# Attention, then routed experts: requesting each expert's rows an expert earlier, moving two transposes, halving the last copy

## The chip, the cores and the metric

The kernel runs on one core of one Trainium2 chip. The metric is device time in microseconds (us) of one launch; lower is better. The core has a matrix engine (TensorE), two engines that read its accumulators (VectorE and ScalarE), GpSimd, which here issues most of the DMA transfers, and sixteen DMA engines. A profile ("trace") is of one execution. The span that it shows is shorter than the reported time of the same execution (250.5 and 252.12).

## The reference, cut to what matters

```python
def reference(**kwargs):
    attn_out = _attn_ref(q, k, v)                  # 8 batches x 8 heads x 576 x 64, keys and values pooled by 8
    x = attn_out.transpose(0, 2, 1, 3).reshape(4608, 512)
    return _moe_ref(x, domain_id, w1, w2)

def _moe_ref(x, domain_id, w1, w2):                # 8 experts, w1 512 x 1024, w2 1024 x 512
    for e in range(8):
        mask = domain_id == e
        h = np.maximum(x[mask] @ w1[e], 0.0)
        out[mask] = h @ w2[e]
```

Every token goes to exactly one expert. The kernel computes the attention, writes the rows x to device memory, and then works through the experts: it gathers the rows of one expert, transposes them, multiplies by w1, applies ReLU, multiplies by w2 and scatters the results to their tokens.

## The kernel before

An expert has room for 640 rows, five blocks of 128. Four kinds of work matter here. A *gather* of one block is an indirect DMA issued by GpSimd. There are two gather buffers, used by even and odd experts. A *turn* is the transposition of one or two gathered blocks on TensorE, followed by a copy to `xT`.

```python
    def gather(e, j, rows=XROWS):
        i = nc.gpsimd.indirect_dma_start(
            out=xg[e % 2][:, j, :], out_offset=None, in_=x_lin[0:rows, :],
            in_offset=bass.IndirectOffsetOnAxis(ap=xrow[:, NBL * e + j:NBL * e + j + 1], axis=0), ...)

    def turn_units(e, j0, j1, tag="big", step=2):
        def unit(a):
            ...
            for j in range(a, z):
                for kk in range(4):
                    nc.tensor.transpose(p[:, j - a, kk, :], xg[e % 2][:, j, 128 * kk:128 * kk + 128], ident[:])
            ...
                nc.vector.tensor_copy(dst, p[:, 0:z - a])      # dst is a part of xT of this expert
```

A *first layer* has eight units of up to eight matmuls; their results are copied to `hT`. A *second layer* has one unit of eight matmuls for each block of 128 rows, a copy to `y`, and a scatter that GpSimd issues.

```python
    def l2_units(e, s0, s1, hT):
        def unit(j):
            p = one(s0 // 128 + j)                             # a PSUM tile of 128 x 512 fp32
            for fi in range(8):
                nc.tensor.matmul(p, hT[:, fi, 128 * j:128 * j + 128], w2[:, fi, :], start=(fi == 0), stop=(fi == 7))
            y = late.tile([128, HD], F32, tag="y", bufs=8, name="y")
            flip[0] ^= 1
            if flip[0]:
                nc.vector.tensor_copy(y[:], p)
            else:
                nc.scalar.activation(y[:], p, AFT.Copy)
            ...                                                # scatter y to out by token, on GpSimd
```

The driver puts the units in order. `paced` interleaves gathers into a first layer: before each one, GpSimd reads one element of `hT`, so it can't run ahead of TensorE.

```python
        run(turn_units(0, 2, 3) + l1_units(0, a, b, h, a))
        run(l2_units(0, 0, b, h) + turn_units(0, 3, NBL))
        run(wload_units(2, 0, 1))
        for j in range(NBL):
            gather(2, j)
        run(l1_units(0, b, CAP, h, b))
        u = l2_units(0, b, CAP, h[:, :, b:CAP])
        t = turn_units(1, 0, NBL)
        run([t[0], u[0], t[1], u[1], t[2]] + wload_units(2, 1, 1))
        for e in range(1, E):
            h = hidden()
            u = l1_units(e, 0, CAP, h, 0)
            ...
            g = [lambda j=j: gather(e + 1, j) for j in range(NBL)] if 2 < e + 1 < E else []
            u = paced(u, h, 0, g, [0, 2, 3, 5, 6])
            run(merge(u, count() if e == 2 else []))
            u = l2_units(e, 0, CAP, h)
            t = turn_units(e + 1, 0, NBL) if e + 1 < E else [lambda: None] * 3
            w = wload_units(e + 2, 0, 1) + wload_units(e + 2, 1, 1) if e + 2 < E else [lambda: None] * 2
            run([u[0], w[0], u[1], t[0], u[2], w[1], t[1], u[3], t[2], u[4]])
```

The softmax here doesn't subtract the row's maximum and nothing guards it: scores larger than these inputs give would overflow.

Of the kernel before, what the change touches and what calls it, by code (L numbers as in the profile page):

```python
# [10 lines left out]
AFT = mybir.ActivationFunctionType  # L11
# [5 lines left out]
HD = 512  # L17
N = B * S
FF = 1024
E = 8  # L20
# [4 lines left out]
NBL = CAP // 128  # L25
# [42 lines left out]
def kernel(  # L68
# [10 lines left out]
    nc = tc.nc  # L79
# [30 lines left out]
    def one(i):  # L110

        if i % 3 != 2:
            return small()[:]
        return wide()[:].rearrange("p a b -> p (a b)")[:, 0:512]
# [24 lines left out]
    with tc.manual_schedule():  # L139
# [447 lines left out]
        def merge(a, b, start=0.0):  # L587

            out_, n = [], len(a)
            pos = [start * n + (i + 0.5) * (1 - start) * n / len(b) for i in range(len(b))] if b else []  # L590
            j = 0
            for i, x in enumerate(a):
                while j < len(b) and pos[j] <= i:
                    out_.append(b[j])
                    j += 1
                out_.append(x)
            return out_ + list(b[j:])
# [6 lines left out]
        def wload_units(e, which, parts):  # L604
            box = {}

            def unit(i):
                if i == 0:
                    tag = W_AT[e % 3][which]
                    k = (4, 8)[which]  # L610
                    t = wp.tile([128, 72, D], F16, tag=tag, bufs=2, name=tag)
                    box["t"] = t[:].rearrange("p t d -> p (t d)")[:, 0:4096].rearrange("p (k f) -> p k f", k=k)
                    box["s"] = (moe_w1, moe_w2)[which][e].rearrange("(k p) f -> p k f", k=k)
                    wt.setdefault(e, []).append(box["t"])
                n = (4, 8)[which] // parts
                nc.gpsimd.dma_start(box["t"][:, n * i:n * i + n], box["s"][:, n * i:n * i + n])
            return [lambda i=i: unit(i) for i in range(parts)]
# [3 lines left out]
# [3 lines that stand above are left out]
                in_offset=bass.IndirectOffsetOnAxis(ap=xrow[:, NBL * e + j:NBL * e + j + 1], axis=0),  # L624
                bounds_check=rows - 1, oob_is_err=False)
            tc.add_to_no_dep_group("xg", i.ins)

        def turn_units(e, j0, j1, tag="big", step=2):
            def unit(a):
                if a == 0:  # L630
                    xts[e] = per.tile([128, 4, CAP], F16, tag="xT", bufs=2, name="xT")
                z = min(a + step, j1)
                p = ps.tile([128, 2, 4, 128], F16, tag=tag, bufs=2, name="turn")
# [3 lines that stand above are left out]
                dst = xts[e][:, :, 128 * a:128 * z].rearrange("p k (j c) -> p j k c", c=128)  # L637
                if tag == "small":
                    nc.scalar.activation(dst, p[:, 0:z - a], AFT.Copy)
                else:  # L640
                    nc.vector.tensor_copy(dst, p[:, 0:z - a])  # L641
            return [lambda a=a: unit(a) for a in range(j0, j1, step)]

        flip = [0]
# [9 lines left out]
        def paced(u, hT, c, fs, at):  # L654
            out_ = []
            for fi, x in enumerate(u):
                out_.append(x)
                out_ += [pace(hT, fi, c, f) for f, i in zip(fs, at) if i == fi]
            return out_

        def hidden():
            return late.tile([128, 8, CAP], F16, tag="hT", bufs=2, name="hT")

        def l1_units(e, s0, s1, hT, h0, alone=False):
            n = s1 - s0
            xT = xts[e]
            w1 = wt[e][0]
            nh = 1 if n <= 512 else 2
            m = n // nh

            def unit(fi):
                p = two(None if alone else fi)
                for kk in range(4):
                    for a in range(nh):
                        nc.tensor.matmul(p[:, a, 0:m], w1[:, kk, 128 * fi:128 * fi + 128], xT[:, kk, s0 + m * a:s0 + m * a + m],  # L675
                                         start=(kk == 0), stop=(kk == 3))
                dst = hT[:, fi, h0:h0 + n].rearrange("p (a c) -> p a c", a=nh)
                if fi % 2 == 0 or alone:
                    nc.scalar.activation(dst, p[:, 0:nh, 0:m], AFT.Relu)  # L679
                else:  # L680
                    nc.vector.tensor_scalar(out=dst, in0=p[:, 0:nh, 0:m], scalar1=0.0, scalar2=None,  # L681
                                            op0=ALU.max)
            return [lambda fi=fi: unit(fi) for fi in range(8)]

        def l2_units(e, s0, s1, hT):
            w2 = wt[e][1]

            def unit(j):
                p = one(s0 // 128 + j)
                for fi in range(8):  # L690
                    nc.tensor.matmul(p, hT[:, fi, 128 * j:128 * j + 128], w2[:, fi, :],  # L691
                                     start=(fi == 0), stop=(fi == 7))
                y = late.tile([128, HD], F32, tag="y", bufs=8, name="y")
                flip[0] ^= 1
                if flip[0]:
                    nc.vector.tensor_copy(y[:], p)  # L696
                else:
                    nc.scalar.activation(y[:], p, AFT.Copy)  # L698
                bl = NBL * e + s0 // 128 + j
                i = nc.gpsimd.indirect_dma_start(  # L700
                    out=out, out_offset=bass.IndirectOffsetOnAxis(ap=orig[0][:, bl:bl + 1], axis=0),
                    in_=y[:], in_offset=None, bounds_check=N - 1, oob_is_err=False)
                tc.declare_no_dep(i.ins, group="ys", reason="each token has its own row")
                tc.add_to_no_dep_group("ys", i.ins)
            return [lambda j=j: unit(j) for j in range((s1 - s0) // 128)]

        def run(units):
            for f in units:
                f()
# [88 lines left out]
        def read_count():  # L798
            nonlocal nblk
            nblk = nc.values_load(nblk_i[0:1, 0:1], min_val=0, max_val=N // 128)  # L800

        a, b = [slots for slots, _ in EARLY]
        h = e0["hT"]
# [4 lines left out]
            gather(1, j)  # L808
        run(wload_units(1, 1, 1))
        run(turn_units(0, 2, 3) + l1_units(0, a, b, h, a))  # L810
        run(l2_units(0, 0, b, h) + turn_units(0, 3, NBL))
        run(wload_units(2, 0, 1))
        for j in range(NBL):
            gather(2, j)
        run(l1_units(0, b, CAP, h, b))
        u = l2_units(0, b, CAP, h[:, :, b:CAP])
        t = turn_units(1, 0, NBL)
        run([t[0], u[0], t[1], u[1], t[2]] + wload_units(2, 1, 1))
        for e in range(1, E):
            h = hidden()  # L820
            u = l1_units(e, 0, CAP, h, 0)
            if e == E - 1:
                nc.gpsimd.drain()
            g = [lambda j=j: gather(e + 1, j) for j in range(NBL)] if 2 < e + 1 < E else []
            u = paced(u, h, 0, g, [0, 2, 3, 5, 6])
            run(merge(u, count() if e == 2 else []))
            u = l2_units(e, 0, CAP, h)
            t = turn_units(e + 1, 0, NBL) if e + 1 < E else [lambda: None] * 3
            w = wload_units(e + 2, 0, 1) + wload_units(e + 2, 1, 1) if e + 2 < E else [lambda: None] * 2
            run([u[0], w[0], u[1], t[0], u[2], w[1], t[1], u[3], t[2], u[4]])  # L830
            if e == 4:
                read_count()
# [3 lines left out]
    with tc.If(nblk > 0), \  # L836
# [8 lines left out]
        with tc.For_i(0, nblk, 1):  # L845
# [37 lines left out]
            with tc.For_i(0, E, 1) as e:  # L883
# [19 lines left out]
                y = ov.tile([128, HD], F32, name="ov_y")  # L903
# [43 lines left out]
```

## Time and profile before

| | |
|---|---|
| timed executions | 250.36, 250.92, 251.54 us; median 250.92 |
| the execution that was traced | 252.12 us, span 250.5 us |
| TensorE busy | 225.0 us, 90% of the span |
| half-clock stretches of TensorE between 12 us and the last matmul | one, of 3.41 us, from 144.9 us |

In timelines below, a row is: start in us, duration in us, engine, source line, operation, output and inputs with shapes, how many instructions are merged, and in brackets the idle time before the row and what ended it. The prediction shows the rows that matter before the change. All of this was read in one execution, and it was slower than the three timed ones.

### The profile page before, as it was taken

Reading aid. Unit: us, or ns where it says so; the run is one execution under the profiler, and the core shown is the slowest. Engines: PE = TensorE matmul, PEld = TensorE weight load, DVE = VectorE, ACT = ScalarE, POOL = GpSimd, SP = SyncE. Lnnn points to the kernel's source line nnn. Section 1 sums busy time; section 2 is a strip of 40 time slices with the busy share of each in tenths; the row PEclk is TensorE's granted clock in tenths of the full one; section 3 lists DMA queues with packets and bytes.
Section 4 is the critical chain, followed back from the end, with each engine's and each line's share of the span. In section 5 each row is a group of like instructions: output and inputs, shape, how many; then the busy total and the mean of one; then the engine's idle time right before and its main releaser. Section 6 shows DMA issues by size and latency. Waiting matters only on the chain.

```text
span 250.5 us, 5043 instructions
## 1 busy us (share of the span) xinstructions
PE 225.0 (90%) x2036; PEld 151.7 (61%) x2036; DVE 119.7 (48%) x267; ACT 96.2 (38%) x163; POOL 139.8 (56%) x190
## 2 busy tenths in 40 slices
PE   4877889999998869889999779999999999999991
PEld 1466668888876656657557346656646656656640
DVE  5874396887987922443334223332343332343320
ACT  8027879869588162203213202312202312203210
POOL 7102999970014037886666547667667677653043
PEclk9999999999999999999999979999999999999997
DMA  5999999999999999699899979949969959942022
GB/s 100 212 219 219 213 216 214 212 223 218 207 350 237 280 297 173 157 144 270 242 194 251 259 163 220 268 100 212 249 166 225 254 117 213 255 155 105 0 105 101
DMA packets 21548, 50.20 MB, mean 200 GB/s; under 512 B 2382, under 2 KB 10640, under 8 KB 20242
## 3 DMA queue, kind: packets, MB, share of 16 engines
q0 software_dynamic: 19712, 45.10, 84.3%
q1 hardware_dynamic: 1810, 4.76, 5.2%
q8 instruction: 16, 0.26, 0.4%
q14 instruction: 10, 0.08, 0.1%
HBM read 67.15 MB, written 15.20 MB: 329 GB/s over the span
## 4 chain that ended last, share of the span: by engine, by line
PE 42%; DMA 27%; issue 9%; POOL 7%; DVE 7%; ACT 6%; POOLq 1%; ACTq 0%
PE small L691 12%; DMA xg<-x_lin,xrow 11%; PE big L675 9%; DMA k<-in_k_dram 9%; POOL out_dram L700 5%; DMA k<-in_moe_w_dram 5%; ACT at L534 4%; PE wide L691 4%; PE wide L675 3%; DMA x_lin<-x_sb 3%; PE turn L636 3%; PE small L459 2%; DVE x_sb L562 2%; PE small L517 2%; PE big L532 2%
## 5 line engine op out<-in xcount | busy, mean ns | idle before, releaser
L700 POOL DMA_INDIRECT out_dram<-y,tok x40 | 40.2, 1005 | 37.7 <-ACT y L698 18.6
L622 POOL DMA_INDIRECT xg<-x_lin,xrow x40 | 41.5, 1038 | 28.9 <-issue 11.9
L691 PEld LDWEIGHTS <-hT 128*128 128x128 f16 x320 | 30.7, 99 | 32.6 <-issue 1.4
L681 DVE TENSOR_SCALAR hT<-big 128x640 f16<-128x640 f32 (+2 forms) x27 | 19.5, 721 | 39.0 <-PE big L675 23.8
L679 ACT ACTIVATE hT<-big 128x640 f16<-128x640 f32 (+2 forms) x32 | 18.6, 584 | 40.3 <-PE big L675 35.9
L698 ACT ACTIVATE y<-small 128x512 f32<-128x512 f32 x16 | 9.6, 597 | 55.9 <-PE small L691 48.9
L534 ACT ACTIVATE at<-big 72x576 f16<-72x576 f32 x42 | 25.9, 655 | 6.6 <-PE big L532 5.7
L675 PEld LDWEIGHTS <-k 128*128 128x128 f16 x224 | 20.6, 98 | 9.0 <-issue 2.4
L675 PE MATMUL big<-xT,k 128*128 128x320 f16 (+2 forms) x164 | 21.8, 280 | 2.5 <-DVE xT L641 1.5
L641 DVE COPY xT<-turn 128x1024 f16<-128x1024 f16 (+1 forms) x23 | 13.7, 594 | 21.6 <-PE turn L636 20.1
L675 PEld LDWEIGHTS <-v 128*128 128x128 f16 x192 | 18.7, 98 | 8.5 <-issue 1.0
L696 DVE COPY y<-small 128x512 f32<-128x512 f32 x16 | 11.1, 692 | 24.1 <-PE small L691 23.2
L691 PE MATMUL small<-q,hT 128*128 128x512 f16 x96 | 22.2, 379 | 0.0
L691 PE MATMUL small<-k,hT 128*128 128x512 f16 x96 | 22.0, 379 | 0.0
L675 PE MATMUL big<-xT,v 128*128 128x320 f16 x144 | 21.2, 299 | 0.8 <-DVE xT L641 0.8
L380 POOL TENSOR_SCALAR op<-iota_f,pos_f 128x128 f16<-128x128 f32 x36 | 21.5, 608 | 0.1
L562 DVE TENSOR_TENSOR x_sb<-big,rcp 128x512 f16<-128x512 f32 x25 | 17.3, 692 | 0.9
L532 PE MATMUL big<-qT,kz 128*72 128x288 f16 x84 | 16.2, 286 | 1.6 <-DVE qT L442 0.8
L636 PE MATMUL turn<-ident,xg 128*128 128x128 f16 x160 | 13.5, 224 | 3.7 <-DMA xg<-x_lin,xrow 3.7
L636 PEld LDWEIGHTS <-xg 128*128 128x128 f16 x160 | 11.0, 100 | 9.7 <-DMA xg<-x_lin,xrow 4.9
L557 PEld LDWEIGHTS <-at 72*128 72x128 f16 (+1 forms) x320 | 14.0, 100 | 4.7 <-issue 1.6
L675 PEld LDWEIGHTS <-q 128*128 128x128 f16 x128 | 12.5, 98 | 5.2
(149 smaller groups left out, 349.0 us busy)
## 6 DMA issues: line engine op xcount, KB each, us to landing
k<-in_moe_w_dram POOLq DMA_DIRECT2D x6, 1024.0 KB
k<-in_k_dram POOLq DMA_DIRECT2D x4, 1152.0 KB
x_lin<-x_sb SPq DMA_DIRECT2D x12, 384.0 KB, 4.6
q<-in_moe_w_dram POOLq DMA_DIRECT2D x4, 1024.0 KB
v<-in_moe_w_dram POOLq DMA_DIRECT2D x4, 1024.0 KB
v<-in_v_dram POOLq DMA_DIRECT2D x3, 1152.0 KB
q<-in_q_dram POOLq DMA_DIRECT2D x3, 1152.0 KB
q<-in_moe_w_dram POOLq DMA_DIRECT2D x2, 512.0 KB
```

The costliest lines, as they stand in the source:

```text
L380: nc.gpsimd.tensor_scalar(out=op[:, c, :], in0=iota_f[:], scalar1=pos_f[:, NC_ * pr + c:NC_ * pr + c + 1], scalar2=None, op0=ALU.is_equal)
L532: nc.tensor.matmul(p[0:72, par, 0:288], s["kpT"][:, par, bh, :], s["qT"][:, :, 8 * bh:8 * bh + 8], start=True, stop=True)
L534: nc.scalar.activation(at[0:72, bh % 8, :].rearrange("p (a c) -> p a c", a=2), p[0:72, :, 0:288], AFT.Exp, scale=1.0 / 64.0)
L557: nc.tensor.matmul(pv[r0:r0 + z - a, h, 0:65], s["at", bt][0:72, h, a:z], s["vp"][0:72, 8 * bt + h, :], start=True, stop=True, skip_group_ ...
L562: nc.vector.tensor_tensor(out=x_sb.rearrange("p (h d) -> p h d", d=D), in0=pv[:, :, 0:64], in1=rcp[:].unsqueeze(2).to_broadcast([128, 8, D ...
L622: i = nc.gpsimd.indirect_dma_start(out=xg[e % 2][:, j, :], out_offset=None, in_=x_lin[0:rows, :], in_offset=bass.IndirectOffsetOnAxis(ap=x ...
L636: nc.tensor.transpose(p[:, j - a, kk, :], xg[e % 2][:, j, 128 * kk:128 * kk + 128], ident[:])
L675: nc.tensor.matmul(p[:, a, 0:m], w1[:, kk, 128 * fi:128 * fi + 128], xT[:, kk, s0 + m * a:s0 + m * a + m], start=(kk == 0), stop=(kk == 3))
L679: nc.scalar.activation(dst, p[:, 0:nh, 0:m], AFT.Relu)
L681: nc.vector.tensor_scalar(out=dst, in0=p[:, 0:nh, 0:m], scalar1=0.0, scalar2=None, op0=ALU.max)
L691: nc.tensor.matmul(p, hT[:, fi, 128 * j:128 * j + 128], w2[:, fi, :], start=(fi == 0), stop=(fi == 7))
L700: i = nc.gpsimd.indirect_dma_start(out=out, out_offset=bass.IndirectOffsetOnAxis(ap=orig[0][:, bl:bl + 1], axis=0), in_=y[:], in_offset=No ...
```

## The change

The intent was to take late gathers off TensorE's path (request them a whole expert earlier, and move the load of the second weights of expert 2 behind them), to let two copies of transposed rows run under matmuls, and to shorten the very last copy by using two engines.

```diff
                 flip[0] ^= 1
-                if flip[0]:
+                if e == E - 1 and s0 // 128 + j == NBL - 1:
+                    nc.vector.tensor_copy(y[:, 0:HD // 2], p[:, 0:HD // 2])
+                    nc.scalar.activation(y[:, HD // 2:HD], p[:, HD // 2:HD], AFT.Copy)
+                elif flip[0]:
                     nc.vector.tensor_copy(y[:], p)
...
-        run(l2_units(0, 0, b, h) + turn_units(0, 3, NBL))
+        u = l2_units(0, 0, b, h)
+        run(u[:-1] + turn_units(0, 3, NBL) + u[-1:])
...
-        run([t[0], u[0], t[1], u[1], t[2]] + wload_units(2, 1, 1))
+        run([t[0], u[0], t[1], t[2], u[1]])
         for e in range(1, E):
...
-            g = [lambda j=j: gather(e + 1, j) for j in range(NBL)] if 2 < e + 1 < E else []
+            g = [lambda j=j: gather(e + 2, j) for j in range(NBL)] if e + 2 < E else []
...
+            if e == 1:
+                run(wload_units(2, 1, 1))
             run([u[0], w[0], u[1], t[0], u[2], w[1], t[1], u[3], t[2], u[4]])
```

Below, "part 1" is the gathers and the moved load, "part 2" the two turns, "part 3" the halves of the last y. "The v load" is the load of the second weights of expert 2.

## The prediction

> **What bounds the kernel now.** I began with the page's list of busy engines, then read the chain of work that ended last, then the timeline of TensorE alone and of GpSimd alone.
>
> ```profile
> PE 225.0 (90%) x2036; PEld 151.7 (61%) x2036; DVE 119.7 (48%) x267; ACT 96.2 (38%) x163; POOL 139.8 (56%) x190
> ```
>
> TensorE is the engine to watch, but 90% is a mean. The change touches only the expert phase, from about 87 us on. There the chain shows one long DMA link that TensorE really sat behind:
>
> ```profile
> 133.15 12.10 DMA xg<-x_lin,xrow
> 145.30 1.04 PE turn L636 x8
> ```
>
> A gather of expert 3 is requested at 133.15 and TensorE transposes its rows at 145.30. (The chain's other long links after 165 us also walk along GpSimd and DMA, but TensorE's timeline has almost no gap there, so I don't count them.) TensorE's own timeline, the rows around every gap that the change can reach:
>
> ```profile
> 99.22 1.89 PE L691 MATMUL wide<-q,hT 128*128 128x512 f16 x8
> 100.94 0.61 PE L636 MATMUL turn<-ident,xg 128*128 128x128 f16 x8
> 102.49 1.03 PE L675 MATMUL big<-xT,k 128*128 128x256 f16 x8 [0.93 <-DVE xT L641]
> ...
> 110.91 0.30 PE L675 MATMUL big<-xT,v 128*128 128x320 f16 x1
> 111.96 2.20 PE L675 MATMUL big<-xT,v 128*128 128x320 f16 x15 [0.75 <-DVE xT L641]
> ...
> 138.96 3.62 PE L691 MATMUL small<-v,hT 128*128 128x512 f16 x16
> 145.30 1.04 PE L636 MATMUL turn<-ident,xg 128*128 128x128 f16 x8 [2.72 <-DMA xg<-x_lin,xrow]
> 146.13 2.98 PE L691 MATMUL wide<-v,hT 128*128 128x512 f16 x8
> 148.94 0.61 PE L636 MATMUL turn<-ident,xg 128*128 128x128 f16 x8
> 149.39 1.89 PE L691 MATMUL small<-v,hT 128*128 128x512 f16 x8
> ...
> 184.06 0.74 PE L636 MATMUL turn<-ident,xg 128*128 128x128 f16 x8 [0.24 <-DMA xg<-x_lin,xrow]
> ```
>
> The bracket is idle time before the row and what ended it. There are two waits for a vector copy of transposed rows and two for gathers. Everywhere else from 112 us to 244.9 us TensorE runs without a gap: one expert takes 18.44 us (153.07 to 171.51 in the same timeline). So here a microsecond of gap removed is a microsecond of time, until something else becomes late. The wait at 145.30 costs twice: the next eight matmuls take 2.98 instead of 1.89. The table of stretches shows why, in its clock column (1.00, 0.93, 0.60, 1.00):
>
> ```profile
> 145.30:149.10 3.80, 3.80 (x19) 2.07 (x20) 0.69 (x1) 0.00 (x0) 2.58 (x3) 0.60 0.58 113
> 149.10:153.00 3.90, 3.90 (x29) 2.08 (x26) 1.71 (x3) 0.60 (x1) 2.58 (x3) 1.00 1.16 186
> ```
>
> **What the Trainium skill says.** "TensorE: Matmul & The Clock Gate", section "The HAM clock gate", says that an idle window of about 3.4 us halves TensorE's clock, and that the window runs freely. The trace agrees: its clock record has one half-rate stretch in the expert phase, 3.41 us long, from 144.9. "DMA: Bandwidth & Descriptors", section "Queues, rings and completion order", says that a ring's descriptors are consumed in ring order; the trace's landing marks of GpSimd's transfers from 121 to 138 us come in order of issue, so here a transfer placed ahead of another delays it. The same page, "Anatomy of one DMA", fits a transfer as 2.0 us plus bytes over 436 GB/s. For a 2 MB weight read that would be 6.8 us; the trace shows 9.7 (below), so I use 9.7. "PSUM — Partial Sum Buffer", section "PSUM bank collisions raise a hardware error", says that ScalarE and VectorE must not read one bank at once and that the compiler's scheduler makes such a pair dependent. The last y is read from 512 fp32 columns, exactly the 2 KiB that this page gives a bank. No row of this trace shows both engines in one bank.
>
> **Part 1, gathers sooner.** It removes the waits at 145.30 and 184.06 if the gathers land in time. Costs counted on TensorE, start to start: second-layer units take 1.725 (8 matmuls), so the two units from 138.96 end their issue at 142.41; the stall to 145.30 is 2.89. Then the turn takes 0.83 (145.30 to 146.13) where 0.45 is usual, and the unit 2.81 (to 148.94) where 1.73 is usual: 0.38 + 1.08. Sum 4.35. At 184.06: issue ends at 180.20 + 3.45 = 183.65, stall 0.41, turn 0.12 longer: 0.53. Together **4.9 us**.
>
> What it adds is on GpSimd. The gathers of expert 3 go into GpSimd's list between the second scatter of expert 0's end and the load of expert 2's second weights (v), and that load is pushed behind the first layer of expert 1:
>
> ```profile
> 119.30 1.01 POOL L700 DMA_INDIRECT out_dram<-y,tok  x1 [0.30 <-issue]
> 121.94 0.95 POOL L616 DMA_DIRECT2D v<-in_moe_w_dram  x1 [1.63 <-DMA q<-in_moe_w_dram]
> ...
> 138.84 1.03 POOL L622 DMA_INDIRECT xg<-x_lin,xrow  x1 [0.15 <-ACT hT L679]
> ```
>
> The load at 121.94 waited for an earlier transfer. The trace names a semaphore per transfer, and GpSimd's transfers take eight in turn, so each waits for the one issued eight before it. In the changed order the first gather of expert 3 inherits that wait: it starts at 121.94. Gathers whose marks are ready follow each other by 1.38 (137.46 to 138.84, 138.84 to 140.21) and last 1.03, so the v load starts at 121.94 + 4 x 1.38 + 1.03 = 128.5 instead of 121.94. In the trace it was issued at 121.94 and its last landing mark came at 131.67, 9.73 later, onto rings nearly empty by 123.3; the other load of that shape onto near-empty rings (104.56) took about 10. After the change the rings are nearly empty again, so I estimate landing at **138.2 to 138.6**. Second layer 2 used it at 138.96; if TensorE comes 1.3 earlier (part 2), it wants it at about 137.7. So a new wait of 0.5 to 0.9 appears exactly there. Expert 3's gathers themselves should land near 130, long before use. The later weights have room: my count along the eight-semaphore rule puts expert 4's first weights at about 161, needed at 166.6.
>
> **Part 2, turns moved ahead.** For expert 1, the last turn goes before the second unit; its copy then runs under 1.73 us of matmuls. Stall now: one matmul after 110.91 (0.14), then nothing until 111.96: **0.9** gained. The gathers it needs landed by 106.3. For expert 0 the stall is 102.49 - 101.39 = 1.1, but the moved turn would start at 99.22, and the landing marks of the last gather it needs come at 100.03 (the one before: 98.99). So TensorE waits about 0.8 at a new place and only **0.3 to 0.5** is gained. Sum 1.3, but the v load caps it: from second layer 2 on, the gain so far is 138.96 less 138.3 to 138.6, say **0.5**.
>
> **Part 3, last y in halves.** Now:
>
> ```profile
> 244.94 0.60 ACT L698 ACTIVATE y<-small 128x512 f32<-128x512 f32 x1 [2.86 <-PEq L836]
> 245.81 0.98 POOL L700 DMA_INDIRECT out_dram<-y,tok  x1 [0.69 <-ACT y L698]
> ```
>
> Half-width rows (256 columns, the hT groups) take 0.42 on VectorE and 0.38 on ScalarE. Side by side that would gain about 0.18. In series, as the bank rule suggests, 0.42 + 0.38 plus a handover of about 0.1 is 0.9: a loss of 0.3. I take **-0.2**.
>
> Sum: 0.5 + 4.9 - 0.2 = 5.2 to 5.4. From 250.92: about 245.6.
>
> **Rivals.** (a) The v load lands well after 139: the stall at 145.30 comes back as a weight wait at second layer 2. For it: GpSimd is busy nearly without a break from 94.7 to 120, and the rings would run near-empty between 124 and 130 while gathers trickle. Against it: the arithmetic puts v within a microsecond of need. One us later is 246.7; if the wait passed some 2.5 us, the half clock could return, and 248 would be the time. (b) The v load comes in time, say in 5 us of transfer, as back-to-back loads of this shape do (137.2 to 142.5 in the DMA records): parts 1 and 2 count in full, and the time is 244.7 or so. (c) GpSimd or the rings become the bound for all experts. Against: 12 transfers per expert, as before; two loads, five gathers and five scatters take about 16.5 us along the eight-semaphore rule, under 18.44, so lateness shrinks by about 2 us per expert. If it went wrong, every expert would stretch and the time would stay near 250. (d) The gathers were hidden anyway: TensorE's 2.72 at 145.30 speaks against it.
>
> **Range and chances.** The 4.9 of part 1 is measured gap and clock, so I trust it; the spread comes from the v load (1 us each way) and the halves (0.25 each way). 2% is 245.9, close to my number, hence the split: 245.6, range 244.5 to 246.9; faster by over 2% 0.60, within 2% 0.38, slower 0.02.
>
> **What would show it.** Right: no gap before expert 3's first turn, no half clock after 140 us until the end; a small gap at the first second-layer matmul of expert 2, released by the v load, with that load issued near 128.5; a wait of up to 0.9 for xg before expert 0's last turn near 99.2; no wait for xT before expert 1's first layer; the two halves of y one after the other. Wrong: a gap over 1.5 us at second layer 2; a first layer waiting for weights anywhere from expert 3 on; evictions waiting for y buffers; or the halves side by side.

## The result

| | times, us | median | ratio to before |
|---|---|---|---|
| before | 250.36, 250.92, 251.43, 251.54 | 251.18 | |
| changed | 247.04, 247.49, 247.75, 248.97 | 247.62 | 0.9871 [0.9823, 0.9919] |

A ratio here and below is the mean time of one kernel's fast runs over the mean of the other's fast runs of the same rounds, so it isn't quite the ratio of the two medians. Brackets are the 95% interval.

The time fell by 1.3%, which counts as the same at a limit of 2%. The prediction said 245.6 with a range of 244.5 to 246.9, so it was wrong: by the medians the gain was 3.3 us (from 250.92) to 3.6 us (from 251.18) where 5.3 was forecast. The traced execution of the changed kernel took 247.49 us, span 245.8.

TensorE's timeline after, the rows that answer to those shown in the prediction:

```profile
87.86 0.40 PE L636 MATMUL turn<-ident,xg 128*128 128x128 f16 x4 [1.87 <-DMA xg<-x_lin,xrow]
88.69 0.50 PE L636 MATMUL turn<-ident,xg 128*128 128x128 f16 x4 [0.43 <-DMA xg<-x_lin,xrow]
...
100.84 0.61 PE L636 MATMUL turn<-ident,xg 128*128 128x128 f16 x8
101.28 1.89 PE L691 MATMUL wide<-q,hT 128*128 128x512 f16 x8
103.01 1.04 PE L675 MATMUL big<-xT,k 128*128 128x256 f16 x8
...
111.34 2.34 PE L675 MATMUL big<-xT,v 128*128 128x320 f16 x16
...
138.94 3.61 PE L691 MATMUL small<-v,hT 128*128 128x512 f16 x16 [0.30 <-DMA v<-in_moe_w_dram]
142.39 0.61 PE L636 MATMUL turn<-ident,xg 128*128 128x128 f16 x8
142.84 1.89 PE L691 MATMUL wide<-v,hT 128*128 128x512 f16 x8
```

Read from the bottom. The first turn of expert 3 (142.39) follows the matmuls without a gap. The two waits for copies, at 103.01 and 111.34, are gone. Second layer 2 (138.94) waits a little for the v load, the new wait that was foreseen. But at the top there is something that the first trace of the kernel before did not have: the first turn of expert 0 waits 1.87 and 0.43 us for its gathers. Neither this turn nor anything ahead of it on TensorE was touched by the change. The half-clock stretch has moved there too. The clock is the third column from the right in this row of the table of stretches:

```profile
89.80:93.30 3.50, 3.43 (x21) 2.65 (x21) 0.00 (x0) 1.50 (x5) 0.69 (x1) 0.65 1.15 297
```

GpSimd's timeline after, where the v load now stands behind five gathers of expert 3:

```profile
118.21 1.01 POOL L703 DMA_INDIRECT out_dram<-y,tok  x1 [0.30 <-issue]
...
122.47 1.06 POOL L622 DMA_INDIRECT xg<-x_lin,xrow  x1 [3.09 <-PE small L691]
...
129.02 0.99 POOL L616 DMA_DIRECT2D v<-in_moe_w_dram  x1
```

The end, after:

```profile
240.04 0.42 DVE L696 COPY y<-small 128x256 f32<-128x256 f32 x1 [1.09 <-PEq L842]
240.50 0.38 ACT L697 ACTIVATE y<-small 128x256 f32<-128x256 f32 x1 [3.32 <-DVE y L696]
241.16 0.98 POOL L703 DMA_INDIRECT out_dram<-y,tok  x1 [0.95 <-ACT y L697]
```

The two halves run one after the other: ScalarE's wait was ended by VectorE's copy. The last group of matmuls ends at 236.33 + 3.62 = 239.95, so the last scatter starts 1.21 us after it. Before, that was 245.81 - 244.86 = 0.95.

So, read against the first trace, the mechanisms of parts 1 and 3 and the new wait for the v load are there with about the size they were given. Only the wait foreseen before expert 0's moved turn is missing (100.84 has no bracket). The two traces even differ by 4.7 us of span (250.5 to 245.8). It was the timed executions that differed by less. The question became whether the first trace of the kernel before showed its usual execution.

### The profile page after: what moved, and what is told of

The parts are those of the page before. It is cut to its first block, busy times and chain, and to the rows that moved or that the text cites. A ratio compares the mean times of both kernels' runs of the same rounds, so it can differ in the third digit from the quotient of the medians.

```text
span 245.8 us, 5065 instructions
## 1 busy us (share of the span) xinstructions
PE 223.6 (91%) x2036; PEld 151.7 (62%) x2036; DVE 120.1 (49%) x268; ACT 96.2 (39%) x163; POOL 139.3 (57%) x190
## 4 chain that ended last, share of the span: by engine, by line
PE 48%; DMA 24%; issue 9%; POOL 7%; ACT 6%; DVE 5%; POOLq 1%; ACTq 0%
PE small L691 14%; PE big L675 13%; DMA k<-in_k_dram 9%; DMA q<-in_moe_w_dram 5%; PE wide L675 5%; PE wide L691 4%; ACT at L534 4%; DMA v<-in_moe_w_dram 4%; DMA xg<-x_lin,xrow 4%; POOL out_dram L703 4%; PE turn L636 2%; PE small L459 2%; DMA x_lin<-x_sb 2%; PE small L517 2%; POOL xg L622 1%
## 5 line engine op out<-in xcount | busy, mean ns | idle before, releaser
L701 ACT ACTIVATE y<-small 128x512 f32<-128x512 f32 x15 | 9.0, 597 | 48.8 <-PE small L691 40.8
L675 PEld LDWEIGHTS <-k 128*128 128x128 f16 x224 | 21.3, 101 | 8.3 <-issue 0.8
L675 PE MATMUL big<-xT,k 128*128 128x320 f16 (+2 forms) x164 | 22.4, 286 | 1.2 <-ACT xT L639 0.7
L534 ACT ACTIVATE at<-wide 72x576 f16<-72x576 f32 x22 | 14.3, 651 | 2.6 <-PE wide L532 2.5
```

What stands on the lines that cost most here:

```text
L534: nc.scalar.activation(at[0:72, bh % 8, :].rearrange("p (a c) -> p a c", a=2), p[0:72, :, 0:288], AFT.Exp, scale=1.0 / 64.0)
L675: nc.tensor.matmul(p[:, a, 0:m], w1[:, kk, 128 * fi:128 * fi + 128], xT[:, kk, s0 + m * a:s0 + m * a + m], start=(kk == 0), stop=(kk == 3))
```

## The experiments

**Two stretches.** To compare traces whose early parts differ, I measured on TensorE's timeline from the start of expert 0's third turn to the start of second layer 2 (stretch 1), and from there to the start of second layer 7 (stretch 2). Stretch 1 holds what the turns can gain, stretch 2 what late gathers cost, and the start of the third turn tells how late TensorE already is. All figures are us, from one traced execution each; with the rounded starts of the rows shown they come out the same to 0.01.

| trace | time of that execution | third turn at | stretch 1 | stretch 2 |
|---|---|---|---|---|
| before, first trace | 252.12 | 92.88 | 46.08 | **97.10** |
| before, second trace | 250.02 | 94.48 | 45.90 | 93.47 |
| before, look 1 | 249.90 | 94.73 | 45.91 | 93.21 |
| before, look 2 | 251.78 | 96.32 | 45.90 | 93.43 |
| before, look 3 | 249.94 | 94.31 | 45.91 | 93.66 |
| before, look 4 | 250.70 | 95.07 | 45.91 | 93.66 |
| part 2 alone | 250.13 | 94.33 | 43.97 | 95.57 |
| part 1 alone | 248.58 | 94.39 | 45.91 | 92.22 |
| parts 1 and 2 | 246.93 | 94.58 | 43.97 | 92.22 |
| changed, first trace | 247.49 | 94.51 | 44.43 | 92.21 |
| changed, second trace | 247.23 | 94.61 | 43.97 | 92.22 |

**Theory A**: the first trace was an unusual execution. TensorE came to expert 0 early and then lost that, and more, at expert 3. Usually it is late already at expert 0 and loses little at expert 3. **Theory B**: the changed order itself causes the early wait.

### The kernel before, traced again

No edit. Timed in five rounds.

> The kernel before, unchanged, once more. Theory A (the execution of before that I read was a slow one, 252.12 us against a median of 251.18, and its stall with half clock at the first turn of expert 3 is larger than usual): this profile has a span of 249 to 249.8 and loses less than 4.35 us there, say 2.5 to 3.5, or has the half clock elsewhere; the mean clocks of its executions differ (about 0.993 without the half-clock stretch, 0.987 with it). Theory B (the changed order costs something early, where the first turn of expert 0 waited 1.9 us for its gather at half clock in the changed kernel only): here the first turn of expert 0 does not wait, in any profile of a kernel with the old order, and the stall at expert 3 is again 2.7 to 3 us with the half clock, 4.3 in all. Ratio to before 1.000.

It took 250.74 us (250.0 to 252.35; ratio 0.9989 [0.995, 1.0028]), span 248.3. TensorE's timeline:

```profile
88.19 1.00 PE L636 MATMUL turn<-ident,xg 128*128 128x128 f16 x8 [2.33 <-DMA xg<-x_lin,xrow]
...
104.08 1.03 PE L675 MATMUL big<-xT,k 128*128 128x256 f16 x8 [0.93 <-DVE xT L641]
...
113.38 2.20 PE L675 MATMUL big<-xT,v 128*128 128x320 f16 x15 [0.75 <-DVE xT L641]
...
140.38 3.62 PE L691 MATMUL small<-v,hT 128*128 128x512 f16 x16
144.29 0.77 PE L636 MATMUL turn<-ident,xg 128*128 128x128 f16 x8 [0.30 <-DMA xg<-x_lin,xrow]
```

Its stretches table at the place of the early wait:

```profile
88.80:92.20 3.40, 2.71 (x16) 1.83 (x15) 0.00 (x0) 1.79 (x4) 1.20 (x2) 0.50 1.12 318
```

The unchanged kernel has the early wait and the early half clock as well, so theory B falls. Theory A's own figures missed too: the span was to be 249 to 249.8 and the loss at expert 3 still 2.5 to 3.5. All of stretch 2 lost only 93.47 - 92.21 = 1.26 against the changed kernel's. Because of them it reaches second layer 2 at 140.38 instead of 138.96. The gather of expert 3 is used at 144.29, where the first trace used it at 145.30. So the stall of 2.89 us (start to start) has shrunk to 0.46, and no half clock follows. Stretch 2 is 93.47 instead of 97.10.

### The kernel before, four more looks

No edit, one traced execution each, on another chip. They came last, to settle which of the two pictures is the usual one.

> The kernel before, one more traced execution of four, to see how its waits are spread. Theory A: most show a wait of 1.5 us or more at the first turn of expert 0 and then a stall under 1 us at the first turn of expert 3 (spans near 248.3); where the early wait is short, the later stall is long, and the sum of what both cost changes less than either. Rival (each execution has about 2.7 us at expert 3, and the second trace was the odd one): 2 us or more at expert 3 in most.

> As the look before it: under theory A an early wait of 1.5 us or more with a stall under 1 us at expert 3; under the rival 2 us or more at expert 3.

> As the looks before it: under theory A an early wait of 1.5 us or more with a stall under 1 us at expert 3; under the rival 2 us or more at expert 3.

> As the looks before it: under theory A an early wait of 1.5 us or more with a stall under 1 us at expert 3; under the rival 2 us or more at expert 3.

A single execution has no state of its own here; the granted clocks, 0.983 to 0.990, lie within those of the fast runs above. All four show an early wait (2.20 and 0.30; 2.95; 1.93 and 0.29; 2.65 us) and a half-clock stretch that begins between 88.2 and 89.7 us. The second is the latest of all:

```profile
88.98 1.07 PE L636 MATMUL turn<-ident,xg 128*128 128x128 f16 x8 [2.95 <-DMA xg<-x_lin,xrow]
...
146.30 0.77 PE L636 MATMUL turn<-ident,xg 128*128 128x128 f16 x8 [0.46 <-DMA xg<-x_lin,xrow]
```

From the end of the matmuls' issue to the first turn of expert 3 the four lose 0.30, 0.63, 1.02 and 0.68 us. In one of them, look 3, this is 0.02 over the expected "under 1 us". With the second trace, five of six traces have a stretch 2 of 93.2 to 93.7, mean 93.49. Only the first has 97.10.

### Part 1 alone

The changed kernel with the turns and the last copy put back (the lines of the last copy are left out here):

```diff
-        u = l2_units(0, 0, b, h)
-        run(u[:-1] + turn_units(0, 3, NBL) + u[-1:])
+        run(l2_units(0, 0, b, h) + turn_units(0, 3, NBL))
-        run([t[0], u[0], t[1], t[2], u[1]])
+        run([t[0], u[0], t[1], u[1], t[2]])
```

> Part 1 alone: gathers a whole expert sooner and the second weights of expert 2 after the first layer of expert 1; turns and last y as before. From the first traces: the v load lands near 138.3 to 138.9, wanted at 138.96, so no new wait or under 0.2 us; the 4.9 us of stalls and half clock go. Theory A: time falls by 3 to 4 us (ratio 0.984 to 0.988), less than 4.9 because the usual execution of before loses less. Theory B: it falls by 4.5 to 5 if its first turn does not wait, and by 3 if it does.

It took 249.17 us, ratio 0.9935 [0.9896, 0.9973]: a gain of about 1.6 us, less than either theory's number. Stretch 2 is 92.22. Against the usual 93.49 that is 1.27 us: all that the gathers cost in a usual execution, not the 3 to 4 that I still expected after one trace.

```profile
140.30 3.62 PE L691 MATMUL small<-v,hT 128*128 128x512 f16 x16
143.75 0.61 PE L636 MATMUL turn<-ident,xg 128*128 128x128 f16 x8
```

No gap at expert 3's first turn, and no wait for the v load.

### Part 2 alone

The kernel before with `u[:-1] + turn_units(0, 3, NBL) + u[-1:]`, and `t[2]` ahead of `u[1]`; nothing else.

> Part 2 alone: the two turns moved ahead of a second-layer unit, all else as before. Both theories: TensorE is 0.9 to 1.9 us earlier at second layer 2, but the first turn of expert 3 still waits for its gather, which lands at the same time, so the stall there grows by what was gained and the time is the same within 0.5 us (ratio 0.998 to 1.002). If instead the time falls by 1 to 1.5 us, the gather is not what sets the time there.

It took 250.64 us, ratio 0.9985 [0.995, 1.002]: nothing that the timed runs resolve. Stretch 1 fell from 45.91 to 43.97, so the turns do save 1.94 us. Stretch 2 took it back, 95.57 instead of 93.49:

```profile
138.31 3.62 PE L691 MATMUL small<-v,hT 128*128 128x512 f16 x16
144.34 0.74 PE L636 MATMUL turn<-ident,xg 128*128 128x128 f16 x8 [2.42 <-DMA xg<-x_lin,xrow]
```

TensorE came 2.07 us sooner than in the second trace of before (138.31 against 140.38), and the turn began at 144.34 against 144.29. The gather landed at the same time although it had been requested 2.07 us sooner (132.50 against 134.57).

The landing marks (the trace's records that a piece of a transfer has arrived; up to 16 for each transfer) show what it stood behind: the load of expert 3's second weights, requested about 5 us ahead of it.

| trace | gather requested | last mark of those weights | last mark of the gather |
|---|---|---|---|
| before, first | 133.15 | 144.21 | 145.25 |
| before, second | 134.57 | 142.76 | 144.25 |
| part 2 alone | 132.50 | 143.28 | 144.30 |

In the changed order this gather is requested ahead of those weights, onto nearly empty rings, and lands 2.87 us after its request (122.47 to 125.34). So in the three traces the gather lands 1.0 to 1.5 us after the weights ahead of it, whenever it was requested. Part 1 changes both its place and its time of request; no run separates the two.

### Parts 1 and 2, without the halves

```diff
-                if e == E - 1 and s0 // 128 + j == NBL - 1:
-                    ...
-                elif flip[0]:
+                if flip[0]:
```

> The changed kernel with the last y copied whole by one engine again. The trace of the changed kernel has the two halves in series, 0.42 and 0.38 with 0.46 from start to start, so the last scatter starts 1.21 us after the last matmul's issue ends against 0.93 before: without the halves the time should be 0.3 us lower than the changed kernel's (about 247.3 where that has 247.6). If the halves mattered more, 1 us lower. Theory A: ratio to before 0.984 to 0.987. Theory B: the same ratio, with a wait of about 2 us and half clock at the first turn of expert 0 again.

It took 247.62 us, ratio 0.9853 [0.9817, 0.9889]. Alone the two parts gave about 1.6 and 0.4 us; together they gave 3.7. Part 2 pays only when part 1 has removed the stall behind it. By the stretches: 1.94 + 1.27 = 3.2 us. The last scatter starts 0.96 us after the last matmul group ends (240.52 - 235.94 - 3.62), as in the kernel before. So the halves cost 0.25 us, which the timed runs can't resolve.

### An added delay, with and without the stall

Nine matmuls of 128x512, results unread, ahead of the first layer of expert 1; once in part 2 alone, once in parts 1 and 2.

```diff
             u = l1_units(e, 0, CAP, h, 0)
+            if e == 1:
+                warm(9, xts[1][:, 0, :])
```

> Part 2 alone, with nine extra 128x512 matmuls (results unread, 9 x 0.216 = 1.94 us) on TensorE just before the first layer of expert 1. Theory A (the gathers of expert 3 land on their own time, so what part 2 saves is idle time there): most of the 1.94 us vanishes in the stall of about 2.4 us at expert 3, and the time rises by only 0 to 0.6 us over part 2 alone (ratio to before 0.998 to 1.001), the stall falling to about 0.5. Rival (that stall is not a meeting point, the gathers move along with TensorE): the time rises by 1.9 us (ratio 1.006).

> The same nine matmuls in the changed kernel without the halves, where no gather and hardly a weight load is waited for. Theory A: the 1.94 us count whole, ratio to before 0.992 to 0.994 where the kernel without them had 0.985. Rival (hidden slack remains, for example at the v load): it rises by under 1 us.

| | without delay | with delay | stretch 1 | stretch 2 |
|---|---|---|---|---|
| part 2 alone | 0.9985 | 0.9999 [0.995, 1.0047] | 43.97 to 45.91 | 95.57 to 93.67 |
| parts 1 and 2 | 0.9853 | 0.9945 [0.9902, 0.9988] | 43.97 to 45.91 | 92.22 to 92.22 |

The ratios with and without come from different chips, each to its own runs of before. In both kernels stretch 1 grew by 1.94. Where the stall was there, stretch 2 gave back 1.90:

```profile
146.14 0.76 PE L636 MATMUL turn<-ident,xg 128*128 128x128 f16 x8 [0.66 <-DMA xg<-x_lin,xrow]
```

Where the stall had been removed, nothing came back, and the time rose by 0.9% (2.3 us, somewhat over the 0.7 to 0.9% expected). This shows the stall for what it is: a meeting point of TensorE and a transfer, which swallows up to its own length of what is lost ahead of it, as it swallowed what part 2 saved. Two limits belong to this. The traced execution of part 2 with the delay also had a longer early half-clock stretch (6.83 us), reached the third turn at 95.95 instead of 94.33, and so came to second layer 2 later by 3.55 us, not 1.94. And the meeting point isn't a fixed appointment: the gather was requested at 136.06 instead of 132.50, because its pacing follows TensorE, and landed 1.8 us later. The stall fell from 2.58 to 0.83 us (start to start). The timed runs are the cleaner evidence: 0.9999 [0.995, 1.0047], where the rival asked for 1.006.

### Idle-time matmuls at the early wait

Eight matmuls of 128x448, results unread, ahead of the first turn of expert 0, where TensorE waits in any case. They should keep its clock up. The list that orders the attention's units gets one more `T` for them (not shown below). Three kernels: before, parts 1 and 2, and the next experiment's.

```diff
+        def filler():
+            p = small()
+            for i in range(8):
+                nc.tensor.matmul(p[:, 0:448], ident[:],
+                                 st[NP - 1]["qT"][:].rearrange("p a b -> p (a b)")[:, 0:448],
+                                 start=True, stop=True, skip_group_check=True)
...
-                    u = turn_units(0, 0, EARLY[0][0] // 128, "small", 1)
+                    u = [filler] + turn_units(0, 0, EARLY[0][0] // 128, "small", 1)
```

> The kernel before with eight idle-time matmuls (128x448, results unread) put ahead of the first turn of expert 0, where four of the five traces since wait about 2 us for a gather and then run 3.4 us at half clock. Theory A (series: the early wait and the stall at expert 3 stand one behind the other, and the gather of expert 3 sets the later time by itself): no half clock near 89, TensorE 1 to 1.7 us earlier at second layer 2, the stall at the first turn of expert 3 grows from 0.3 to 1.5 to 2 us, and the time stays within 0.5 us of before (ratio 0.998 to 1.002). Theory B (the two are independent): the time falls by 1.5 us (ratio 0.994).

In the kernel before: 251.41 us (median of six runs, one of them slow), ratio of the fast runs 0.9976 [0.9928, 1.0024]. The clock stayed at 1.00, the third turn came at 93.18, and the stall was long again. From this kernel's stretches table (clock third from the right) and TensorE's timeline:

```profile
88.80:92.20 3.40, 2.71 (x28) 2.32 (x26) 0.00 (x0) 2.44 (x7) 1.02 (x2) 1.00 1.09 327
```

```profile
145.42 0.77 PE L636 MATMUL turn<-ident,xg 128*128 128x128 f16 x8 [2.56 <-DMA xg<-x_lin,xrow]
```

This makes the first trace's picture on purpose: early at expert 0, stalled at expert 3. In the trace nothing was won (last matmul group ends at 243.84; 242.65 to 244.45 in the five usual traces). The timed ratio can't decide it: its interval holds the 0.998 to 1.002 of theory A and the 0.994 of its rival. Theory A expected a stall of 1.5 to 2; it was 2.56. Stretch 2 is 95.80, and the half clock did not follow this time. The first trace had 97.10 with it.

> The same eight matmuls in the changed kernel without the halves. Theory A: TensorE comes to second layer 2 at about 137 instead of 138.5, but its v load, issued near 128.2, lands at 137.7 to 138.9, so a wait of 0.7 to 1.8 us appears there and only 0 to 0.8 us is gained (time 246.8 to 247.6). Theory B: 1.5 us gained (246.1).

> Both: v first, and the eight matmuls ahead of the first turn of expert 0. Theory A: with neither the gather of expert 3 nor the v load in the way, the 1 to 1.7 us of the avoided half clock come through whole: 245.8 to 246.6, the fastest so far (ratio to before 0.979 to 0.983). Theory B: no more than the filler gave alone in the kernel before.

In the other two kernels: 249.19 us, ratio 0.9848 [0.9779, 0.9917], and 247.83 us, ratio 0.9845 [0.9797, 0.9893]. Without the eight matmuls these kernels have 0.9853 and 0.9866. So the gain of over 1 us, which theory A expected at least with v first (0.979 to 0.983), isn't seen, though that interval doesn't rule it out. This chip was also the noisiest of the four; its runs of before went from 250.63 to 260.02 us, two of eleven slow, and so were two of the six runs behind the 249.19. The traces give a reason. The third turn still came at 94.91 and 94.29, after a wait of 0.24 and 0.19 us for its own gather, and the first layer behind it then waited twice for copies (0.36 and 0.34; 0.51 and 0.33). Stretch 1 was 44.98 and 45.06 instead of 43.97: about 1 us was lost right behind the place where the half clock was avoided. The wait of 0.7 to 1.8 us for the v load that theory A expected in parts 1 and 2 did not come. How much of the early half clock can be won back this way stays open.

### The v load ahead of the gathers

Against parts 1 and 2:

```diff
-        run([t[0], u[0], t[1], t[2], u[1]])
+        run([t[0], u[0], t[1], t[2], u[1]] + wload_units(2, 1, 1))
...
-            if e == 1:
-                run(wload_units(2, 1, 1))
```

> The changed kernel without the halves, with the second weights of expert 2 requested before the gathers of expert 3 instead of after them. The v load is issued near 121 again and lands near 131; the gathers of expert 3 land behind it, at 132 to 134, long before 142. Theory A: any wait at second layer 2 is gone; as that wait was 0 to 0.5 us in the traces, the time is 0 to 0.5 us below the kernel without the halves (247.1 to 247.6). If a gather were late in this order, a new wait would stand at the first turn of expert 3.

It took 248.65 us (one of six runs slow), ratio of the fast runs 0.9866 [0.981, 0.9923], not to be told from 0.9853. The load was issued at 122.00 instead of about 128.2. Nothing waited for it, nor for the gathers of expert 3. In the traces of the other order the wait for this load was 0.46 us once (the changed kernel's first trace) and zero in three (part 1 alone, parts 1 and 2, the changed kernel's second trace). So there is next to nothing to win. In this execution of the kernel with v first, the first gathers came early (first turn at 87.04), there was no early half clock, and the third turn waited instead:

```profile
93.70 0.40 PE L636 MATMUL turn<-ident,xg 128*128 128x128 f16 x4 [1.31 <-DMA xg<-x_lin,xrow]
```

It is the same pattern once more, one gather further up.

### The changed kernel again

No edit.

> The changed kernel once more. Theory A (the usual execution of before loses only about 1.3 us to late gathers, since it is late already at expert 0; the change gains about 1.8 us by the turns, 0.7 at expert 3 and 0.65 at expert 5, and loses 0.3 by the halves): ratio to before 0.986 to 0.989, span 245.3 to 246.3; the two halves in series, 0.42 and 0.38 us, the last scatter about 1.2 us after the last matmul's issue ends; a wait of 0 to 0.6 us for the v load at second layer 2. Theory of the prediction (4.9 us by the gathers in every execution): ratio 0.979.

It took 248.11 us, ratio 0.9903 [0.9856, 0.995], span 245.6; the ratio is just over the expected 0.986 to 0.989, and its interval covers it. Stretches 43.97 and 92.22, no wait for the v load, the halves in series again.

### A version with a narrower last step

V first, turns moved, gathers sooner, and the last block computed as two column halves in two PSUM tiles (PSUM is the memory that TensorE's results land in). The diff shows the last block only. The first half is copied while TensorE does the second.

```diff
+                last = e == E - 1 and s0 // 128 + j == NBL - 1
+                for c in ((0, HD // 2) if last else (0,)):
+                    z = c + HD // 2 if last else HD
+                    p = (small()[:] if last else one(s0 // 128 + j))[:, 0:z - c]
+                    for fi in range(8):
+                        nc.tensor.matmul(p, hT[:, fi, 128 * j:128 * j + 128], w2[:, fi, c:z],
+                                         start=(fi == 0), stop=(fi == 7))
+                    if last and c == 0:
+                        nc.vector.tensor_copy(y[:, c:z], p)
+                    elif last:
+                        nc.scalar.activation(y[:, c:z], p, AFT.Copy)
...
```

> v first, turns moved, gathers sooner, and the very last block computed as two column halves in two separate banks, so that the first half is copied while TensorE does the second: after the last matmul only a 256-column copy of 0.38 us remains, instead of 0.60 (whole) or 0.84 (two halves of one bank in series). Theory A: 0.2 us under the kernel without the halves, 0.5 us under the changed kernel: ratio to before 0.983 to 0.986; in the trace the last scatter starts 0.65 to 0.75 us after the last matmul's issue ends. If the sixteen narrow matmuls cost TensorE time, the last block takes more than 1.8 us.

```profile
238.67 0.42 DVE L698 COPY y<-small 128x256 f32<-128x256 f32 x1 [0.24 <-PE small L695]
...
239.60 0.38 ACT L700 ACTIVATE y<-small 128x256 f32<-128x256 f32 x1 [2.94 <-PEq L846]
240.26 0.98 POOL L709 DMA_INDIRECT out_dram<-y,tok  x1 [0.57 <-ACT y L700]
```

Its last group of matmuls ends at 235.81 + 3.70 = 239.51. The last scatter starts 0.75 us later, against 0.96 with one whole copy and 1.21 with two halves of one tile. The sixteen narrow matmuls cost 0.08 us (second layer 7 to the end of the matmuls: 8.88 against 8.80). It took 247.54 us, ratio 0.9882 [0.9841, 0.9923], where the changed kernel in the same rounds had 248.11 and 0.9903. Expected was 0.983 to 0.986, a miss, though the interval reaches into it. Its interval lies below 1, so it beats the kernel before, by less than 2%. That it beats the changed kernel by about 0.4 us at the end is in the traces; the timed runs don't show it.

## Why the prediction was wrong, point by point

**The step that failed: "The 4.9 of part 1 is measured gap and clock, so I trust it".** It was measured, but in one execution that was not the usual one. The stretches give exactly this number for that execution (97.10 - 92.21 = 4.89). In the five other traces of the same kernel it is 93.49 - 92.22 = 1.27. Usually the first gather of expert 0 lands later (last mark at 87.56 to 88.93, in the first trace 86.89) while TensorE is done with the attention sooner (its last matmul row before the turn starts at 85.23 to 85.60, there 86.60). TensorE waits for the gather, runs 3.4 us or more at half clock, and comes to second layer 2 later by 1.3 to 3.3 us. So most of the stall at expert 3 isn't left to be removed: it is 0.30 to 1.02 us instead of 2.89. The half clock behind it, another 0.38 + 1.08 us of the 4.9, didn't come there in any of the five. What the first trace offered as one cost at 145 us was mostly a delay of TensorE that usually is spent at 88 us, where the change does nothing. The time of the traced execution, 252.12 us against 250.36 to 251.54, was a weak sign at most: look 2 took 251.78 with the usual picture.

**"The v load caps it ... say 0.5" for part 2.** This had the same root. With TensorE usually later, second layer 2 wants the v load at about 138.5, and it landed at 137.5 to 137.7 in two traces and at 138.9 in one. So the cap took 0.46 us once and nothing otherwise, and part 2 gave 1.94 us (in the changed kernel's first trace 46.08 - 44.43 = 1.65 against the first trace of before), not 0.5. The wait of about 0.8 us foreseen before expert 0's moved turn did not come either: the turn was reached at 100.84, after its gather had landed (99.73 by the landing marks).

**Right in place and size.** The issue of the v load (129.02; 128.5 was said). Its 9.88 us to landing (9.73 was used). The new wait for it in the changed kernel's first trace (0.46; 0.5 to 0.9 was said). The removal of both copy waits and of every gather wait from expert 3 on. The halves one after the other, 0.25 us lost (0.2 was taken). No weight came late anywhere after, and no y buffer ran out.

**The sum as it should have been**: 1.27 + 1.94 - 0.25 = 2.96 us from usual executions, 248.2 from the median of 251.18. The two errors have opposite signs (3.6 too much in part 1, 1.4 too little in part 2); that the forecast was no further off is luck. The two timed comparisons gave ratios of 0.9871 and 0.9903, that is about 3.2 and 2.4 us. That stays inside 2%. The forecast chance of "faster by over 2%", 0.60, came from setting a sum of 5.3 against a limit of 5.0, with 4.9 of it resting on one trace. Rivals (a) to (c) asked whether the change would create a new wait. Only (d), that the gathers were hidden anyway, asked about the old one, and it was set aside with the same single trace.

**What stays open.** Why the first gathers of expert 0 come early in some executions is not shown. They are requested at 78.1 to 78.4 in all six traces of before, about 4 us behind a weight load, and that load's last mark varies too (86.60 in the first trace, 86.86 to 88.15 in the others).

The half clock after the stall at expert 3 came in one of the three traces with a stall of over 2.4 us (first trace of before; not in part 2 alone, nor with the eight matmuls). The traces suggest why. Up to the last matmul, the granted clock changes in all 18 of them only at whole steps of 3.413 us from its first rise. I added up TensorE's idle time step by step. After every step at full clock with 1.84 us or more of idle time the clock fell (15 steps), and after none with 1.65 us or less (1179 steps). The first trace's gap put 2.32 us into the step from 141.49 to 144.90. In the other two a step ended inside the gap and left 1.65 and 0.77, and 1.59 and 0.97. The steps start at a different time in each execution (11.78, 10.45 and 11.34 in these three), so whether a stall of this length brought the half clock would depend on where it fell. No run moved a gap on purpose to test this.

## What to carry to other kernels

Before a wait in a trace is counted as a gain, trace the same kernel several times: a stall at a meeting point of an engine and a transfer depends on how early the engine happens to come (0.30 to 2.89 us in six traces here). Look, too, at what stands ahead of the transfer: here part 1, which requested the gather ahead of a weight load, removed the stall. Two savings on such a path don't add: here one alone gave nothing that could be timed, the other 1.6 us, and together they gave 3.7 us. Two engines copying halves of one PSUM tile ran one after the other here and lost 0.25 us; halving the last step into two tiles, filled one after the other, gained 0.21 less 0.08 for the narrower matmuls. Whether the bank or the shared tile `y` put the copies in series was not separated.

## What the Trainium skill lacked or had wrong

- "TensorE: Matmul & The Clock Gate", section "The HAM clock gate", gives an idle window of about 3.4 us for the drop to half clock. Here it followed shorter waits: all 13 traces with a single wait of 1.6 to 3.0 us around 88 us have a half-clock stretch there. It followed a wait of 2.72 us at 145 us, but not waits of 2.42 and 2.56 us at the same place. The window need not be idle throughout: the clock fell after every step of 3.413 us with 1.84 us or more of idle time in it and after none with 1.65 or less (18 traces). The page lacks this amount. The length of a stretch, 3.41 us (6.83 in two traces), agrees with it.
- "DMA: Bandwidth & Descriptors", section "Anatomy of one DMA", fits 2.0 us plus bytes over 436 GB/s, about 6.8 us for a 2 MB read. A weight load of 2 MB that is written as 1 MB of another type, onto nearly empty rings, took 9.2 to 10.4 us from issue to landing (the v load in 15 traces; 9.73 in the first of before, 9.88 in the first of the changed kernel). The page has no separate figure for a load that converts its type.
- "PSUM — Partial Sum Buffer", section "PSUM bank collisions raise a hardware error", agrees with what was seen: the two copies of one bank ran in series, 0.46 us from start to start. It doesn't name the cost, which here made the split 0.25 us slower than one whole copy.
- The profiling pages that I read, "Perfetto Trace Analysis" among them, don't say that one trace may be of an unusual execution. Six traces of one kernel had 97.10, 93.47, 93.21, 93.43, 93.66 and 93.66 us for the same stretch of the same program.
